# Attention decode with a gated feed-forward: V of a head in one transfer with 48 KB a partition, K in halves of the same rows

## The chip, the core and the metric

The kernel runs on one core of one Trainium2 chip. A core has a matrix engine (TensorE, PE in the profile), a vector engine (VectorE, DVE), a scalar engine (ScalarE, ACT), GpSimd (POOL) and a sync engine (SyncE, SP), which here only issues DMA transfers. Sixteen DMA engines carry data from the device memory into the on-chip memory of 128 partitions. The metric is the device time of one execution in microseconds.

## What is computed

One token of width 640 goes through a layer norm, multi-head attention over a cache, a residual, a second layer norm, a gated feed-forward layer and a second residual, all in float32:

```python
B, Sq, D = 1, 1, 640
H, Sk, Dh = 32, 8192, 192          # F = 1536
q = (layernorm(x) @ wq).reshape(B, Sq, H, Dh).transpose(0, 2, 1, 3)
scores = einsum("bhqd,bhkd->bhqk", q, k_cache) * Dh ** -0.5
o = einsum("bhqk,bhkd->bhqd", softmax(scores), v_cache)
h = x + o.transpose(0, 2, 1, 3).reshape(B, Sq, H * Dh) @ wo
n = layernorm(h)
gate = n @ W_gate
out = h + (gate * (gate > 0) * (n @ W_up)) @ W_down
```

K and V of one head are 8192 x 192 numbers each, 6.3 MB. The whole input is 446 MB, nearly all of it K and V, and each byte of them is used once.

## The kernel before

**Layout.** A head's 8192 cache positions are cut into two chunks of 4096 (`NCH = 2`). In a chunk each of the 128 partitions holds 32 positions that follow each other (`R = 32`), so a chunk is one tile of 128 rows of 24 KB, and each row is one contiguous piece of memory. `load_kv` (L77 to L83) loads such a chunk of K or V with one transfer of 3072 KB; the very last chunk of V comes in four quarters. All these tiles, the five slices of the query weights at the start and the feed-forward weights at the end share the pool `kv` with six buffers. The output weights have their own pool `wts` with two buffers.

**Start.** SP asks for the five slices of the query weights (L74). ACT asks for x twice: once with five numbers in each partition (`xT`), once as one row (`xrow`). After the layer norm, PE computes all 32 queries (L159), and ACT copies them out (`q4`). Four matmuls with a row of ones (L149) put x into the accumulator `acc`, as the residual.

**One head.** `query(h)` spreads the query of a head over all partitions in PSUM (L168). `scores_of` (L171) multiplies each half of a K chunk with it on DVE, in place (L178), and sums over the 192 columns: ten positions of each sixteen on DVE (L179), six on ACT (L181). `softmax_of` (L185) finds the maximum over all partitions with a transposition (L189) and a broadcast (L193) on PE, takes the exponential on ACT (L198) and sums with a matmul (L200). `values_of` (L212) multiplies with V: 32 matmul pairs of 384 columns, which the trace shows as 64 matmul records (L217); the first half of them reads V's chunk 0, the second chunk 1. ACT scales the result (L220). `to_columns` (L223) turns it so that it can be multiplied with the output weights, with matmuls (L232) and a transposition on DVE (L235). Heads go in groups: seven groups of four (0 to 27), then 28 and 29, then 30 and 31. When a group is complete, `output_of` (L237) multiplies with the output weights of the group and adds into `acc` (L241); the last two heads do so one by one.

**The loop** (L246 to L266) is software-pipelined by one head. In its pass h stand, in this order: at the first head of a group, the load of the group's output weights (`load_wo`, L90); the loads of K(h+1) chunk 0, V(h) chunk 0, K(h+1) chunk 1, V(h) chunk 1; the query of head h+1; the values of head h; scores and softmax of head h+1; `to_columns` of head h; and at the end of a group `output_of`.

**What sets the order.** All large loads are issued by SP on one queue. Each waits on SP until its buffer is free: for a K buffer, until DVE and ACT have summed the chunk that was in it; for a V buffer, until PE has multiplied it; for the output weights, until the last matmul of `output_of` that read the buffer. A load that waits keeps those behind it waiting. The transfers that are issued run on the 16 DMA engines, each engine taking 8 of the 128 rows of every transfer. The framework that builds the kernel places the instructions on each engine's queue and puts in the waits; for a pool with n buffers, the (n+1)th tile waits for the first to be released.

**End.** After the last head come the feed-forward weights (L275 to L290): up in two transfers, gate in three, down in four, in the same six buffers. Meanwhile PE, ACT and DVE finish `acc`, take the second layer norm (L293 to L313), compute up and gate (`project`, L315), combine and turn them (L329, L331) and compute the down projection in twelve slices as they land (L337). Two queues store the result (L343).

Of the kernel before, what the change touches and what calls it, by code (L numbers as in the profile page):

```python
# [7 lines left out]
F32 = mybir.dt.float32  # L8
# [6 lines left out]
def kernel(  # L15
# [23 lines left out]
    TW = R * DH  # L39
# [3 lines left out]
    DG = D // NQ  # L43
# [21 lines left out]
    xrow = const.tile([1, D], F32, name="xrow")  # L65
    nc.scalar.dma_start(xT, x[0, 0].rearrange("(p j) -> p j", p=P))
    nc.scalar.dma_start(xrow, x[0])


    wq_v = wq.rearrange("(p j) n -> p j n", p=P)  # L70
    wq_ts = []
    for j in range(DJ):
        t = kv.tile([P, TW], F32, name="kv_t")
        nc.sync.dma_start(t, wq_v[:, j, :])  # L74
        wq_ts.append(t)

    def load_kv(src, h, c, parts=1):  # L77
        t = kv.tile([P, TW], F32, name="kv_t")
        v = src[h, c * P * R:(c + 1) * P * R, :].rearrange("(p r) d -> p (r d)", p=P)
        n = TW // parts  # L80
        for i in range(parts):
            nc.sync.dma_start(t[:, i * n:(i + 1) * n], v[:, i * n:(i + 1) * n])
        return t  # L83

    def load_wo(gi):
        hs = GROUPS[gi]
        j = len(hs) * DH // P
        t = wts.tile([P, j, D], F32, tag="wo_t", name="wo_t")
        r0 = hs[0] * DH
        nc.sync.dma_start(t, wo[r0:r0 + len(hs) * DH, :].rearrange("(p j) n -> p j n", p=P))  # L90
        return t

    ones = const.tile([P, P], F32, name="ones")
# [3 lines left out]
    ident = const.tile([P, P], F32, name="ident")  # L97
# [73 lines left out]
    def scores_of(q, kts):  # L171
        sc = small.tile([P, NS], F32, name="sc")
        for c, kt in enumerate(kts):
            k3 = kt.rearrange("p (r d) -> p r d", d=DH)
            for r0 in range(0, R, SUB):
                ks = k3[:, r0:r0 + SUB, :]
                i0 = c * R + r0
                nc.vector.tensor_mul(ks, ks, q[:, None, :].to_broadcast([P, SUB, DH]))  # L178
                nc.vector.reduce_sum(sc[:, i0:i0 + SUB - NA], ks[:, :SUB - NA, :], axis=AX.X)  # L179
# [29 lines left out]
        nc.vector.memset(po, 0.0)  # L209
    NP = NS // 2  # L210

    def values_of(h, p, rl, vts):  # L212
        po = pos[h % 2]
        for i in range(NP):
            c, r = divmod(2 * i, R)
            g = i % NQ
            nc.tensor.matmul(po[g * Q:g * Q + 2, :], p[:, 2 * i:2 * i + 2],  # L217
                             vts[c][:, r * DH:(r + 2) * DH], start=(i < NQ), stop=(i >= NP - NQ))
        ob = small.tile([P, 2 * DH], F32, name="ob")
        nc.scalar.activation(ob, po, AF.Copy, scale=rl)  # L220
        return ob
# [19 lines left out]
                nc.tensor.matmul(acc[g * Q:(g + 1) * Q, :], oT[s, j, :], wo_t[s, j, g * DG:(g + 1) * DG],  # L241
                                 start=False, stop=(last and j == J - 1))

    kts = [load_kv(kf, 0, c) for c in range(NCH)]
    sm = softmax_of(scores_of(query(0), kts))
    for h in range(H):  # L246
        gi, i = group_of[h]
        hs = GROUPS[gi]
        if i == 0:
            wo_t = load_wo(gi)  # L250
            oT = small.tile([P, len(hs) * DH // P, Q], F32, tag="oT", name="oT")
        vts, kts = [], []
        for c in range(NCH):
            if h + 1 < H:
                kts.append(load_kv(kf, h + 1, c))
            vts.append(load_kv(vf, h, c, 4 if h == H - 1 and c == NCH - 1 else 1))
        if h + 1 < H:
            q = query(h + 1)
        ob = values_of(h, *sm, vts)
# [20 lines left out]
    up_b, gt_b = rest[:, 0:F], rest[:, F:2 * F]  # L280
    dn_b = rest[:, 2 * F:2 * F + 3 * D].rearrange("p (j n) -> p j n", n=D)
    dn_c = dn_a[:, 0:9 * D].rearrange("p (j n) -> p j n", n=D)
    nc.sync.dma_start(up_a, rows_of(w_up)[:, 0:JA, :])
    nc.sync.dma_start(up_b, rows_of(w_up)[:, JA, :])
    nc.sync.dma_start(gt_a[:, 0:2, :], rows_of(w_gate)[:, 0:2, :])
    nc.sync.dma_start(gt_a[:, 2:4, :], rows_of(w_gate)[:, 2:4, :])
    nc.sync.dma_start(gt_b, rows_of(w_gate)[:, JA, :])
# [24 lines left out]
    hr = row.tile([P, 1], F32, name="hr")  # L312
    rstd_of(hr, hvar, "h")  # L313

    def project(ps, wa, wb):  # L315
        for j in range(DJ):
            w = wa[:, j, :] if j < JA else wb
# [5 lines left out]
    project(pu, up_a, up_b)  # L323
# [3 lines left out]
    project(pg, gt_a, gt_b)  # L327
# [6 lines left out]
    for j in range(FJ):  # L334
        w = dn_b[:, j, :] if j < 3 else dn_c[:, j - 3, :]
        for g in range(NQ):
            nc.tensor.matmul(pd[g * Q:(g + 1) * Q, 0:DG], guT[:, j, :], w[:, g * DG:(g + 1) * DG],  # L337
                             start=(j == 0), stop=(j == FJ - 1))
# [32 lines left out]
```

## Time and profile before

| | |
|---|---|
| median of 3 runs | 1055.49 us (1055.3 to 1055.65) |
| the profiled execution | 1055.67 us, of which 1053.9 us is the span from the first to the last instruction |
| instructions | 8860 |
| granted TensorE clock, mean | 0.669 |
| data packets and bytes | 22374 packets, 446.48 MB, 424 GB/s over the span |

The page of the profile gives the busy time of each engine, then the span in 40 slices of 26.3 us with the busy share of the DMA engines and the GB/s that they moved, then the DMA queues, then the chain of work that ended last. Two more views are used. The DMA view can be cut to a stretch of time and then gives the packets, bytes and mean rate in it ("under 512 B" counts the short packets that report a transfer's completion, one for each of the 16 engines that took part). The timeline gives, for each instruction or run of equal ones, start, duration, engine, line, operation, tiles and shape, "x" and the count, and in brackets how long the engine had been idle before and what ended that. "SPq" marks SP's issue of a transfer. In the table of windows the last two numbers of a line are the DMA engines' busy share and the GB/s.

### The profile page before, as it was taken

To read this page: it belongs to the slowest core of one execution; us is meant where nothing else is said; L and a number is where in the kernel's file an instruction comes from. 1 tells how busy PE (TensorE), PEld (TensorE's weight loads), DVE (VectorE), ACT (ScalarE), POOL (GpSimd) and SP (SyncE) were. 2 spreads that over 40 slices of the span, in tenths; PEclk is the share of its full clock that TensorE was granted. 3 is DMA by queue.
4 is the path that set the end of the run, shared out by engine and by line. 5 is a ranking of instruction groups with operands and counts; after the bars stand their busy time and mean duration, and the time that the engine had idled before them with its cause. 6 is when DMAs were issued, how large, how long until landed. Compare 5 with 4: busy or idle time off the path is not lost.

```text
span 1053.9 us, 8860 instructions
## 1 busy us (share of the span) xinstructions
PE 439.4 (42%) x3136; PEld 135.6 (13%) x3136; DVE 727.0 (69%) x418; ACT 325.1 (31%) x1676; POOL 1.9 (0%) x11
## 2 busy tenths in 40 slices
PE   3523444344434333433442444344325433532466
PEld 1101111111111010111110111111101101100122
DVE  1188877677867777687776777677875877687641
ACT  0043333223323332232232333233332333333230
POOL 0000000000000000000000000000000000000000
PEclk9656666666676666766666665766667666666666
DMA  9999999999999999999999999999999999999995
GB/s 391 431 428 432 433 430 430 427 431 428 430 431 430 430 430 428 431 429 431 429 430 430 432 431 429 428 428 430 431 429 433 430 428 427 435 428 429 431 418 231
DMA packets 22374, 446.48 MB, mean 424 GB/s; under 512 B 2613, under 2 KB 2617, under 8 KB 4154
## 3 DMA queue, kind: packets, MB, share of 16 engines
q1 hardware_dynamic: 22180, 445.92, 99.0%
q8 instruction: 24, 0.39, 0.2%
q14 instruction: 20, 0.16, 0.0%
q10 hardware_dynamic: 150, 0.01, 0.0%
HBM read 445.91 MB, written 0.00 MB: 423 GB/s over the span
## 4 chain that ended last, share of the span: by engine, by line
DMA 62%; DVE 28%; PE 8%; issue 1%; ACT 1%; SPq 0%; DVEq 0%
DMA kv_t<-in_A_k_cache_dram 57%; DVE kv_t L178 19%; DVE sc L179 7%; PE po L217 5%; DMA up_a<-in_B_W_up_dram 3%; DMA dn_a<-in_B_W_down_dram 2%; PE q L168 1%; PE ps_small L232 1%; ACT p L198 0%; PE ps_small L193 0%; PE ps_small L200 0%; DVE oT L235 0%; DVE m L191 0%; SPq L74 0%; PE ps_small L189 0%
## 5 line engine op out<-in xcount | busy, mean ns | idle before, releaser
L178 DVE TENSOR_TENSOR kv_t<-kv_t,q 128x3072 f32<-128x3072 f32 x128 | 423.3, 3347 | 165.7 <-DMA kv_t<-in_A_k_cache_dram 165.1
L181 ACT ACTIVATE kv_t<-kv_t 128x192 f32<-128x192 f32 x768 | 267.7, 349 | 528.8 <-DVE kv_t L178 528.8
L217 PE MATMUL po<-kv_t,p 128*2 128x384 f32 x2048 | 296.7, 749 | 249.1 <-DMA kv_t<-in_A_v_cache_dram 249.1
L179 DVE TENSOR_REDUCE sc<-kv_t 128x10 f32<-128x1920 f32 x128 | 269.0, 2142 | 0.0
L168 PE MATMUL q<-q,sel 128*128 128x192 f32 x64 | 31.0, 589 | 285.6 <-DVE kv_t L178 285.6
L181 ACT ACTIVATION_READ_ACCUMULATOR kv_t<-kv_t 128x1 f32 x768 | 143.3, 187 | 0.0
L217 PEld LDWEIGHTS po<-kv_t,p 128*2 128x2 f32 x2048 | 60.5, 111 | 453.0 <-DMA kv_t<-in_A_v_cache_dram 274.6
L168 PEld LDWEIGHTS q<-q,sel 128*128 128x128 f32 x64 | 15.6, 303 | 316.5 <-DVE kv_t L178 242.2
L220 ACT ACTIVATE ob<-po,rl 128x384 f32<-128x384 f32 x32 | 18.6, 580 | 111.8 <-PE po L217 111.8
L202 DVE RECIPROCAL rl<-ps_small 128x1 f32<-128x1 f32 x32 | 5.4, 168 | 52.6 <-PE ps_small L200 52.6
L191 DVE TENSOR_REDUCE m<-ps_small 1x1 f32<-1x128 f32 x32 | 8.9, 279 | 40.5 <-PE ps_small L189 40.5
L235 DVE STREAM_TRANSPOSE oT<-ps_small 32x192 f32<-32x192 f32 (+1 forms) x32 | 11.7, 367 | 27.0 <-PE ps_small L232 27.0
L232 PE MATMUL ps_small<-ob,par 128*32 128x192 f32 (+1 forms) x144 | 25.6, 314 | 0.7 <-ACT ob L220 0.7
L159 PE MATMUL qp<-kv_t,xn 128*32 128x512 f32 x120 | 21.0, 862 | 11.1 <-DMA kv_t<-in_A_wq_dram 10.1
L200 PE MATMUL ps_small<-rs,ones 128*128 128x1 f32 x64 | 12.4, 264 | 24.9 <-ACT p L198 24.9
L241 PE MATMUL acc<-wo_t,oT 128*32 128x160 f32 (+1 forms) x408 | 18.2, 330 | 4.6 <-DVE oT L235 4.6
L193 PE MATMUL ps_small<-m,ones 1*128 1x1 f32 x64 | 12.3, 259 | 11.9 <-DVE m L191 11.9
L241 PEld LDWEIGHTS acc<-wo_t,oT 128*32 128x32 f32 (+1 forms) x408 | 13.2, 119 | 9.3 <-DVE oT L235 7.8
L200 PEld LDWEIGHTS ps_small<-rs,ones 128*128 128x128 f32 x64 | 9.7, 191 | 27.6 <-ACT p L198 27.6
L193 PEld LDWEIGHTS ps_small<-m,ones 1*128 1x128 f32 x64 | 9.6, 186 | 18.2 <-DVE m L191 18.2
L232 PEld LDWEIGHTS ps_small<-ob,par 128*32 128x32 f32 x144 | 11.3, 109 | 4.8 <-ACT ob L220 1.4
L198 ACT ACTIVATE p<-sc,nb 128x64 f32<-128x64 f32 x32 | 11.1, 348 | 1.2 <-ACT nb L195 0.2
(77 smaller groups left out, 80.3 us busy)
## 6 DMA issues: line engine op xcount, KB each, us to landing
kv_t<-in_A_k_cache_dram SPq DMA_DIRECT2D x64, 3072.0 KB, 33.7
kv_t<-in_A_v_cache_dram SPq DMA_DIRECT2D x63, 3072.0 KB, 39.8
kv_t<-in_A_wq_dram SPq DMA_DIRECT2D x5, 3072.0 KB, 13.9
wo_t<-in_A_wo_dram SPq DMA_DIRECT2D x7, 1920.0 KB, 41.5
kv_t<-in_A_v_cache_dram SPq DMA_DIRECT2D x4, 768.0 KB, 38.8
up_a<-in_B_W_up_dram SPq DMA_DIRECT2D x1, 3072.0 KB, 33.9
gt_a<-in_B_W_gate_dram SPq DMA_DIRECT2D x2, 1536.0 KB
dn_a<-in_B_W_down_dram SPq DMA_DIRECT2D x3, 960.0 KB, 22.7
```

The lines of the kernel that those rows point to most:

```text
L159: nc.tensor.matmul(qps[b][g * Q:(g + 1) * Q, :], xn[:, j:j + 1].to_broadcast([P, Q]), wq_ts[j][:, c0:c0 + QB], start=(j == 0), stop=(j == ...
L168: nc.tensor.matmul(q[:, 0:DH], sel[:, g, :], q4[:, i * DH:(i + 1) * DH], start=True, stop=True)
L178: nc.vector.tensor_mul(ks, ks, q[:, None, :].to_broadcast([P, SUB, DH]))
L179: nc.vector.reduce_sum(sc[:, i0:i0 + SUB - NA], ks[:, :SUB - NA, :], axis=AX.X)
L181: nc.scalar.activation(ks[:, r, :], ks[:, r, :], AF.Copy, accum_out=sc[:, i0 + r:i0 + r + 1])
L193: nc.tensor.matmul(pb[:, 0:1], ones[0:1, :], m1, start=True, stop=True)
L200: nc.tensor.matmul(pl[:, 0:1], ones, rs, start=True, stop=True)
L217: nc.tensor.matmul(po[g * Q:g * Q + 2, :], p[:, 2 * i:2 * i + 2], vts[c][:, r * DH:(r + 2) * DH], start=(i < NQ), stop=(i >= NP - NQ))
L220: nc.scalar.activation(ob, po, AF.Copy, scale=rl)
L232: nc.tensor.matmul(pt[q0:q0 + Q, 0:W], par[:, k, :], ob[:, k * DH + u * W:k * DH + (u + 1) * W], start=(k == 0), stop=(k == 1))
L235: nc.vector.transpose(oT[s], pt[s, 0:W].rearrange("p (c j) -> p j c", c=Q))
L241: nc.tensor.matmul(acc[g * Q:(g + 1) * Q, :], oT[s, j, :], wo_t[s, j, g * DG:(g + 1) * DG], start=False, stop=(last and j == J - 1))
```

## The change

V gets the layout of a whole head: each partition holds 64 positions that follow each other, 48 KB in one row, and one transfer of 6144 KB fetches them. The value matmuls read the same position pairs out of one tile. K must match the positions of V, so a K tile is now the first or the second half (24 KB) of the same 48 KB row. The pool `kv` of six 24 KB buffers becomes `kp` with three 24 KB buffers and `vp` with two 48 KB buffers; V's last head comes as one half and four quarters. The loads stand in the order K(h+1) half 0, K(h+1) half 1, V(h).

The query weights come as two transfers of two slices (48 KB a partition) in the `vp` buffers and one single slice in a `kp` buffer. The up weights come as one transfer of 30 KB a partition, the gate weights as 18 KB and 12 KB.

The pool of the output weights has one buffer in place of two. The load of a group moves from the group's first head to its third (`i == 2`); for the group of heads 28 and 29 it stands at the top of head 28, for the last group behind the load of V(30).

The residual x is loaded as four rows of 160 numbers and enters `acc` through four matmuls that select a row with a column of the identity, in place of a row of ones.

```diff
-    kv = ctx.enter_context(tc.tile_pool(name="kv", bufs=6))
-    wts = ctx.enter_context(tc.tile_pool(name="wts", bufs=2))
+    kp = ctx.enter_context(tc.tile_pool(name="kp", bufs=3))
+    vp = ctx.enter_context(tc.tile_pool(name="vp", bufs=2))
+    wts = ctx.enter_context(tc.tile_pool(name="wts", bufs=1))
...
-    nc.scalar.dma_start(xrow, x[0])
+    nc.scalar.dma_start(xq[0:NQ, :], x[0].rearrange("o (g n) -> (o g) n", g=NQ))
...
-    for j in range(DJ):
-        t = kv.tile([P, TW], F32, name="kv_t")
-        nc.sync.dma_start(t, wq_v[:, j, :])
-        wq_ts.append(t)
-
-    def load_kv(src, h, c, parts=1):
-        t = kv.tile([P, TW], F32, name="kv_t")
-        v = src[h, c * P * R:(c + 1) * P * R, :].rearrange("(p r) d -> p (r d)", p=P)
-        n = TW // parts
-        for i in range(parts):
-            nc.sync.dma_start(t[:, i * n:(i + 1) * n], v[:, i * n:(i + 1) * n])
+    for j in range(0, DJ, 2):
+        n = min(2, DJ - j)
+        t = vp.tile([P, 2 * TW], F32, name="v_t") if n == 2 else kp.tile([P, TW], F32, name="k_t")
+        t3 = t.rearrange("p (j n) -> p j n", n=TW)
+        nc.sync.dma_start(t3, wq_v[:, j:j + n, :])
+        wq_ts += [t3[:, i, :] for i in range(n)]
+
+    def load_k(h, c):
+        t = kp.tile([P, TW], F32, name="k_t")
+        nc.sync.dma_start(t, kf[h].rearrange("(p r) d -> p (r d)", p=P)[:, c * TW:(c + 1) * TW])
+        return t
+
+    def load_v(h, parts=1):
+        t = vp.tile([P, 2 * TW], F32, name="v_t")
+        v = vf[h].rearrange("(p r) d -> p (r d)", p=P)
+        b = 0
+        for n in parts:
+            nc.sync.dma_start(t[:, b:b + n], v[:, b:b + n])
+            b += n
         return t
...
-        nc.tensor.matmul(acc[g * Q:(g + 1) * Q, :], ones[0:1, 0:Q], xrow[:, g * DG:(g + 1) * DG],
+        nc.tensor.matmul(acc[g * Q:(g + 1) * Q, :], ident[0:NQ, g:g + 1].to_broadcast([NQ, Q]), xq[0:NQ, :],
                          start=True, stop=False)
...
             nc.tensor.matmul(po[g * Q:g * Q + 2, :], p[:, 2 * i:2 * i + 2],
-                             vts[c][:, r * DH:(r + 2) * DH], start=(i < NQ), stop=(i >= NP - NQ))
+                             vt[:, 2 * i * DH:(2 * i + 2) * DH], start=(i < NQ), stop=(i >= NP - NQ))
...
         if i == 0:
+            oT = small.tile([P, len(hs) * DH // P, Q], F32, tag="oT", name="oT")
+        if i == 2 or h == 28:
             wo_t = load_wo(gi)
-            oT = small.tile([P, len(hs) * DH // P, Q], F32, tag="oT", name="oT")
-        vts, kts = [], []
-        for c in range(NCH):
-            if h + 1 < H:
-                kts.append(load_kv(kf, h + 1, c))
-            vts.append(load_kv(vf, h, c, 4 if h == H - 1 and c == NCH - 1 else 1))
+        kts = [load_k(h + 1, c) for c in range(NCH)] if h + 1 < H else []
+        vt = load_v(h, [2 * TW] if h + 1 < H else [TW] + [TW // 4] * 4)
+        if h == 30:
+            wo_t = load_wo(gi)
         if h + 1 < H:
             q = query(h + 1)
...
-    JA = 4
-    up_a = kv.tile([P, TW], F32, tag="kv_t", name="up_a").rearrange("p (j n) -> p j n", n=F)
-    gt_a = kv.tile([P, TW], F32, tag="kv_t", name="gt_a").rearrange("p (j n) -> p j n", n=F)
-    dn_a = kv.tile([P, TW], F32, tag="kv_t", name="dn_a")
-    rest = kv.tile([P, TW], F32, tag="kv_t", name="rest")
...
-    nc.sync.dma_start(up_a, rows_of(w_up)[:, 0:JA, :])
-    nc.sync.dma_start(up_b, rows_of(w_up)[:, JA, :])
-    nc.sync.dma_start(gt_a[:, 0:2, :], rows_of(w_gate)[:, 0:2, :])
-    nc.sync.dma_start(gt_a[:, 2:4, :], rows_of(w_gate)[:, 2:4, :])
-    nc.sync.dma_start(gt_b, rows_of(w_gate)[:, JA, :])
+    JA = DJ - 3
+    big = vp.tile([P, 2 * TW], F32, tag="v_t", name="ffn_a")
+    gt_b = kp.tile([P, TW], F32, tag="k_t", name="gt_b")[:, 0:JA * F].rearrange("p (j n) -> p j n", n=F)
+    dn_c = kp.tile([P, TW], F32, tag="k_t", name="dn_c")[:, 0:9 * D].rearrange("p (j n) -> p j n", n=D)
+    up = big[:, 0:DJ * F].rearrange("p (j n) -> p j n", n=F)
+    gt_a = big[:, DJ * F:(DJ + 3) * F].rearrange("p (j n) -> p j n", n=F)
+    dn_b = kp.tile([P, TW], F32, tag="k_t", name="dn_b")[:, 0:3 * D].rearrange("p (j n) -> p j n", n=D)
+    nc.sync.dma_start(up, rows_of(w_up))
+    nc.sync.dma_start(gt_a, rows_of(w_gate)[:, 0:3, :])
+    nc.sync.dma_start(gt_b, rows_of(w_gate)[:, 3:DJ, :])
     nc.sync.dma_start(dn_b, rows_of(w_down)[:, 0:3, :])
```

More of the change, by code (lines that the diff above doesn't have):

```diff
@@ L64 @@
     xT = const.tile([P, DJ], F32, name="xT")
-    xrow = const.tile([1, D], F32, name="xrow")
+    xq = const.tile([Q, DG], F32, name="xq")
     nc.scalar.dma_start(xT, x[0, 0].rearrange("(p j) -> p j", p=P))
-    nc.scalar.dma_start(xrow, x[0])
+    nc.scalar.dma_start(xq[0:NQ, :], x[0].rearrange("o (g n) -> (o g) n", g=NQ))
     wq_v = wq.rearrange("(p j) n -> p j n", p=P)
     wq_ts = []
-    for j in range(DJ):
-        t = kv.tile([P, TW], F32, name="kv_t")
-        nc.sync.dma_start(t, wq_v[:, j, :])
-        wq_ts.append(t)
-    def load_kv(src, h, c, parts=1):
-        t = kv.tile([P, TW], F32, name="kv_t")
-        v = src[h, c * P * R:(c + 1) * P * R, :].rearrange("(p r) d -> p (r d)", p=P)
-        n = TW // parts
-        for i in range(parts):
-            nc.sync.dma_start(t[:, i * n:(i + 1) * n], v[:, i * n:(i + 1) * n])
+    for j in range(0, DJ, 2):
[15 more added lines that the diff above has]
+            b += n
         return t
@@ L242, in output_of @@
                                  start=False, stop=(last and j == J - 1))
-    kts = [load_kv(kf, 0, c) for c in range(NCH)]
+    kts = [load_k(0, c) for c in range(NCH)]
     sm = softmax_of(scores_of(query(0), kts))
@@ L273, in rows_of @@
         return w.rearrange("(p j) n -> p j n", p=P)
-    JA = 4
-    up_a = kv.tile([P, TW], F32, tag="kv_t", name="up_a").rearrange("p (j n) -> p j n", n=F)
-    gt_a = kv.tile([P, TW], F32, tag="kv_t", name="gt_a").rearrange("p (j n) -> p j n", n=F)
-    dn_a = kv.tile([P, TW], F32, tag="kv_t", name="dn_a")
-    rest = kv.tile([P, TW], F32, tag="kv_t", name="rest")
-    up_b, gt_b = rest[:, 0:F], rest[:, F:2 * F]
-    dn_b = rest[:, 2 * F:2 * F + 3 * D].rearrange("p (j n) -> p j n", n=D)
-    dn_c = dn_a[:, 0:9 * D].rearrange("p (j n) -> p j n", n=D)
-    nc.sync.dma_start(up_a, rows_of(w_up)[:, 0:JA, :])
-    nc.sync.dma_start(up_b, rows_of(w_up)[:, JA, :])
-    nc.sync.dma_start(gt_a[:, 0:2, :], rows_of(w_gate)[:, 0:2, :])
-    nc.sync.dma_start(gt_a[:, 2:4, :], rows_of(w_gate)[:, 2:4, :])
-    nc.sync.dma_start(gt_b, rows_of(w_gate)[:, JA, :])
+    JA = DJ - 3
[8 more added lines that the diff above has]
+    nc.sync.dma_start(gt_b, rows_of(w_gate)[:, 3:DJ, :])
     nc.sync.dma_start(dn_b, rows_of(w_down)[:, 0:3, :])
@@ L313, with project @@
     rstd_of(hr, hvar, "h")
-    def project(ps, wa, wb):
+    def project(ps, row_of):
         for j in range(DJ):
-            w = wa[:, j, :] if j < JA else wb
+            w = row_of(j)
             for g in range(NQ):
@@ L322 @@
     pu = ps_q.tile([P, QB], F32, tag="q", name="pu")
-    project(pu, up_a, up_b)
+    project(pu, lambda j: up[:, j, :])
     us = row.tile([P, FG], F32, name="us")
@@ L326 @@
     pg = ps_q.tile([P, QB], F32, tag="q", name="pg")
-    project(pg, gt_a, gt_b)
+    project(pg, lambda j: gt_a[:, j, :] if j < 3 else gt_b[:, j - 3, :])
     gu = row.tile([P, FG], F32, name="gu")
```

5 lines of the change are left out of this document (2 added, 3 removed).

## The prediction

> **What bounds the kernel now.** I read the page from the top, then the chain that ended last, then the DMA view cut to two windows.
>
> ```profile
> PE 439.4 (42%) x3136; PEld 135.6 (13%) x3136; DVE 727.0 (69%) x418; ACT 325.1 (31%) x1676; POOL 1.9 (0%) x11
> GB/s 391 431 428 432 433 430 430 427 431 428 430 431 430 430 430 428 431 429 431 429 430 430 432 431 429 428 428 430 431 429 433 430 428 427 435 428 429 431 418 231
> q1 hardware_dynamic: 22180, 445.92, 99.0%
> DMA 62%; DVE 28%; PE 8%; issue 1%; ACT 1%; SPq 0%; DVEq 0%
> ```
>
> The busiest compute engine, DVE, works 69% of the span. The DMA engines are busy 99.0% of it on the one queue that carries the data, and every slice but the first and the last two moves 427 to 435 GB/s. The chain's 28% on DVE only shows whose work freed a buffer for the next load: the loads stand in line behind others anyway. So the time is 445.92 MB at about 430 GB/s, and an edit counts in two ways only: it changes the time that the engines need for the bytes, or it makes the queue run dry.
>
> ```profile
> DMA packets 12060, 257.99 MB, mean 430 GB/s; under 512 B 1338, under 2 KB 1338, under 8 KB 1338
> q1 hardware_dynamic: 12036, 257.68, 100.3%
> DMA packets 536, 4.24 MB, mean 424 GB/s; under 512 B 56, under 2 KB 56, under 8 KB 378
> q1 hardware_dynamic: 536, 4.24, 101.5%
> ```
>
> These are the DMA view's packet lines for 300 to 900 us (almost all 24 KB rows) and for 1026 to 1036 us (feed-forward weights in 6 to 12 KB rows). **What a packet costs.** In the first there are 12036 - 1338 = 10698 data packets of 24.09 KB (thousand bytes) on average; at 430/16 = 26.9 GB/s an engine, 0.896 us each. In the second 480 packets of 8.83 KB at 26.5 GB/s, 0.333 us each. The straight line through both has 36.9 ns per KB and an intercept of 7 ns; with the busy shares (100.3% and 101.5%) in place of the rates it is 13 ns. I take 10 ns for each packet that goes away, and 7 and 13 as ends.
>
> **The change, part by part: fewer packets.**
>
> ```profile
> kv_t<-in_A_v_cache_dram SPq DMA_DIRECT2D x63, 3072.0 KB, 39.8
> kv_t<-in_A_v_cache_dram SPq DMA_DIRECT2D x4, 768.0 KB, 38.8
> kv_t<-in_A_wq_dram SPq DMA_DIRECT2D x5, 3072.0 KB, 13.9
> gt_a<-in_B_W_gate_dram SPq DMA_DIRECT2D x2, 1536.0 KB
> ```
>
> A transfer has 128 rows, 8 for each engine. V goes from 63 whole transfers and 4 quarters to 31 of double rows, one half and 4 quarters: (63 - 32) x 8 = 248 packets fewer per engine. The query weights go from 5 transfers to 3: 16 fewer. Up goes from 2 to 1, gate from 3 to 2: 8 fewer each. That is 280 x 10 ns = 2.8 us. The transfers themselves fall by 31 + 2 + 1 + 1 = 35, each with one small completion packet per engine; at between nothing and the same 10 ns this is 0 to 0.35 us, I take 0.2. **Sum: 3.0 us saved**, between 2.0 and 4.0 by the ends above. No run shows a 48 KB packet: if it is cut in two it saves nothing, so 0 is the lower end.
>
> Is there more to win from fewer transfers? The window of 300 to 900 us holds 1338/16 = 84 transfers and is 100.3% busy; half a per cent that the share hides would be 36 ns for each, 1.2 us for 35. The Trainium skill ("DMA: Bandwidth & Descriptors", section "Anatomy of one DMA") gives every DMA a fixed 2.0 us beside its bytes; an estimate by it for 35 fewer is 70 us saved where the rows give at most 1.2. This trace disagrees: 84 times 2.0 us would leave 168 of the 600 us idle, and none are.
>
> K in halves of one row reads 24 KB pieces out of 48 KB rows. The old gate transfers already read 12 KB out of 30 KB rows in the window at 424 GB/s, and the query weights 24 KB out of 120 KB rows in the first two slices, of which the second has 431: I take nothing.
>
> **Does the queue stay fed?**
>
> ```profile
> 876.24 6.62 DVE L178 TENSOR_TENSOR kv_t<-kv_t,q 128x3072 f32<-128x3072 f32 x2 [3.00 <-DMA kv_t<-in_A_k_cache_dram]
> 882.78 4.21 DVE L179 TENSOR_REDUCE sc<-kv_t 128x10 f32<-128x1920 f32 x2
> 890.92 6.62 DVE L178 TENSOR_TENSOR kv_t<-kv_t,q 128x3072 f32<-128x3072 f32 x2
> 898.18 5.15 PE L217 MATMUL po<-kv_t,p 128*2 128x384 f32 x32 [7.71 <-DMA kv_t<-in_A_v_cache_dram]
> 1015.73 6.98 PE L217 MATMUL po<-kv_t,p 128*2 128x384 f32 x64
> ```
>
> At 430 GB/s 3072 KB take 7.3 us, so a head takes 29.3: K, K, then V whole. Let K(h+1,0) land at 0; K(h+1,1) lands at 7.3, V(h) at 21.9. The 64 value matmuls of a head took 6.98 us where they ran in one piece (L217 x64), and stand in front of the softmax on PE's queue: they end at 29.4. DVE then needs the softmax (887.0 to 890.9, about 4 us) and 10.75 us per K half, so head h+1's first half is done near 14.5 and its second near 25.2. The third K buffer gives the first half's place to K(h+2,1), whose bytes are due at 29.3: 14 us in hand. K(h+3,0) has 25 us, V(h+1) 21 (issued right behind K(h+2,1)). The values now come later than before, and this margin hides it; without it, every microsecond would cost 32 times. Both margins I cost at nothing, this one and that of the first heads:
>
> ```profile
> 48.54 6.62 DVE L178 TENSOR_TENSOR kv_t<-kv_t,q 128x3072 f32<-128x3072 f32 x2 [32.84 <-DMA kv_t<-in_A_k_cache_dram]
> 55.08 4.21 DVE L179 TENSOR_REDUCE sc<-kv_t 128x10 f32<-128x1920 f32 x2
> ```
>
> K(0,0) is scored from 48.5 to 59.3, and K(1,1) needs its buffer. K(0,0) landed near 48, so K(0,1) and K(1,0) last until 48 + 2 x 7.3 = 62.6; with 1.0 us from issue to bytes (below) there are 2 us in hand.
>
> The output weights of heads 0 to 27 are asked for two heads (58 us) after their one buffer is free, those of heads 30 and 31 behind V(30), 29.3 us after V(29), and the buffer is free 13 us after V(29) (below). **Heads 28 and 29 are different.** Their load stands at the top of head 28, in front of K(29,0), and its one buffer is held until the last output matmul of head 27. That needs V(27), the last transfer in front of it in the same queue. So SP waits with nothing behind V(27) in flight: the DMA engines run dry.
>
> ```profile
> 873.31 0.33 SPq L82 DMA_DIRECT2D kv_t<-in_A_k_cache_dram  x1
> 873.73 0.38 SPq L82 DMA_DIRECT2D kv_t<-in_A_v_cache_dram  x1
> 874.16 0.42 SPq L90 DMA_DIRECT2D wo_t<-in_A_wo_dram  x1
> 999.17 0.33 SPq L284 DMA_DIRECT2D rest<-in_B_W_up_dram  x1
> 1009.94 0.33 SPq L285 DMA_DIRECT2D gt_a<-in_B_W_gate_dram  x1
> 1015.67 0.33 SPq L287 DMA_DIRECT2D rest<-in_B_W_gate_dram  x1
> SPq L285 <- DVE sc L179: 10.4, 1, 10.4
> ```
>
> The queue keeps the order of the program even where a later load could go: gt_a waited 10.4 us for its buffer (SP's own waits) while L287, into a tile that was already placed at 999.17, stayed behind it; and wo_t at 874.16, whose second buffer was free, stands behind the K and V of the head before, which had waited.
>
> ```profile
> 912.14 1.01 PE L168 MATMUL q<-q,sel 128*128 128x192 f32 x2 [8.82 <-DVE kv_t L178]
> 913.08 4.53 PE L217 MATMUL po<-kv_t,p 128*2 128x384 f32 x32
> 920.92 1.84 PE L241 MATMUL acc<-wo_t,oT 128*32 128x160 f32 x48 [0.48 <-DVE oT L235]
> 0.74 2.96 SPq L74 DMA_DIRECT2D kv_t<-in_A_wq_dram  x5
> 0.00:1.00 1.00, 0.00 (x0) 0.00 (x0) 0.16 (x2) 0.00 (x0) 0.47 (x6) 1.00 0.00 0
> 1.00:2.00 1.00, 0.00 (x0) 0.00 (x0) 0.77 (x4) 0.24 (x1) 0.92 (x4) 1.00 1.16 295
> 2.00:3.00 1.00, 0.00 (x0) 0.00 (x0) 0.00 (x0) 1.00 (x1) 0.51 (x3) 1.00 0.43 98
> 1047.00:1048.00 1.00, 1.00 (x20) 0.77 (x16) 0.00 (x0) 0.00 (x0) 0.00 (x0) 0.50 0.06 23
> 1048.00:1049.00 1.00, 0.58 (x12) 0.02 (x3) 0.00 (x0) 0.00 (x0) 0.00 (x0) 0.50 0.04 15
> 1049.08 1.83 PE L337 MATMUL pd<-dn_a,guT 128*32 128x160 f32 x24 [0.50 <-DMA dn_a<-in_B_W_down_dram]
> ```
>
> **The price of the dry stretch**, from V(27)'s last byte to the next byte: landing to first matmul 0.5 us (the last bytes flow before 1049, PE starts at 1049.08); the 64 value matmuls 7.0 (two pieces of 5.15 would be 10.3, the upper end; one piece at the rate of the second half of 4.53 + 4.53 gives 9); from their end to the end of the output matmuls 922.76 - 917.61 = 5.15 (the softmax of head 28, the copy of the values, the transposition); SP's issue to the first byte 1.0 (issue at 0.74, bytes in the window from 1 to 2); and a slow restart: the window from 2 to 3 us moved 98 GB/s, so 0 to 1.4 us, I take 0.5. **Sum: 14.2 us**, between 11 and 18. Nothing hides it: the stream is the bound, everything behind it moves by as much. What is late next is K(29,0), and DVE with it. At the end only one engine of 16 still moves bytes (share 0.06 at 1047), so one engine lags; V(27) too has landed only when this one is done, so its full wait counts.
>
> **Start and end.** The query weights' pairs end with the single fifth transfer, which still lands fifth, and K(0,0) lands when it did. The 4-row matmul for x stands beside the weights' transfer. At the end up, gate and down follow V(31) in the old order with the same bytes; two gate rows come last in place of one, 8 matmuls or about 0.7 us more, in front of the first down group:
>
> ```profile
> 1042.29 1.21 PE L337 MATMUL pd<-rest,guT 128*32 128x160 f32 x24 [1.64 <-DVE guT L331]
> 1044.41 1.83 PE L337 MATMUL pd<-dn_a,guT 128*32 128x160 f32 x24 [0.91 <-DMA dn_a<-in_B_W_down_dram]
> ```
>
> The second group waits 0.91 us for its bytes, which covers it. Nothing.
>
> **Sum.** The profiled execution took 1055.67 us for a span of 1053.9; the median of the runs, 1055.49, is 0.02% lower, so I add to the median: 1055.5 - 3.0 + 14.2 = **1066.7 us**.
>
> **The rivals.** (1) *Faster*: the wait at head 28 doesn't empty the queue, because the order of issue comes out otherwise (K(29) in front of the output weights) or the buffer is free in time. It decides from the point where 14.2 us of bytes, two K halves, stand in front of that load. Then 1055.5 - 3.0 = 1052.5 us. Against it are the rows of SP's order; for it, only that PE's order does differ from the program's (the query of L168 at 912.14 stands between the two halves of a head's values). 10%. (2) 48 KB rows win nothing, because they are cut or run at the old rate: 1055.5 + 14.2 = 1069.7. 15%. (3) A margin fails too, for instance K(1,1)'s 2 us or a per-head one: it would cost from some 3 us once, 1070, to 32 us at 1 us a head. 5%. (4) Each transfer has a fixed gap of its own, and dropping 35 saves it 35 times: by the 1.2 us above 1065.5, inside my range and counted with the forecast. By the Trainium skill's 2.0 us for each, an estimate, it would be about 1000 us; under 1%.
>
> **How the numbers follow.** Forecast 69%, rivals as above. The range takes the gap's ends: 1055.5 - 4.0 + 11 = 1062.5 and 1055.5 + 18 = 1073.5; rival (1) lies outside with 10%. A difference of 0.2%, about 2 us, is what a measurement of this kernel can tell from no change. Faster by more 10%, within 3% (the gap hidden and the rows worth nothing), slower 87%.
>
> **What would show it.** One wait of SP at the output weights' load, over 30 us long, released by PE's output matmul; one slice of the GB/s line between 900 and 930 us at about half; the other slices 431 to 432; about 17,300 packets in place of 22374; DVE waiting some 25 us for K once. No dip, or several, make the prediction wrong, and so does a data rate in the middle that is below 430.

## The result, and the profile after

| | before | changed |
|---|---|---|
| median | 1055.57 us (4 runs) | 1164.15 us (4 runs, 1162.47 to 1165.67) |
| ratio, 95% interval | | 1.103 [1.1016, 1.1044] |
| span of the profiled execution | 1053.9 us | 1162.5 us |

The change costs 108.6 us. The forecast was 11 us slower: the direction is right, the size ten times too small, and the time lies far outside the range.

First the page of the changed kernel, in the parts that were quoted of before: busy times, GB/s in 40 slices (now of 29 us), the data queue, and the shares of the chain that ended last.

```profile
PE 402.4 (35%) x3136; PEld 143.8 (12%) x3136; DVE 723.8 (62%) x418; ACT 325.0 (28%) x1676; POOL 1.9 (0%) x11
GB/s 403 421 422 431 440 430 404 364 412 360 383 405 358 415 381 350 356 432 416 379 357 353 410 375 419 366 366 411 369 355 368 419 416 368 273 252 434 431 337 323
DMA packets 17340, 446.48 MB, mean 384 GB/s; under 512 B 2056, under 2 KB 2064, under 8 KB 3344
q1 hardware_dynamic: 17140, 445.92, 90.9%
DVE 61%; PE 27%; DMA 6%; ACT 3%; issue 2%; SPq 0%; DVEq 0%
```

The packets went as forecast (17340; forecast about 17,300), and no engine has much more to do than before: DVE is busy for 723.8 us (727.0 before), ACT for 325.0 (325.1), PE's matmuls for 402.4 (439.4); only PE's weight loads take a little longer (143.8 against 135.6). But from the seventh slice to the 34th the stream runs at 350 to 432 GB/s: a loss in every head. The single dip that was forecast is there as well, in the slices of 273 and 252, but it is not where the time went (e8 below). DMA had 62% of the chain that ended last; now it has 6%, and DVE and PE have 88%. So the kernel is no longer bound by the bytes, nor by the work of one engine (DVE is busy 62%), but by a chain that runs back and forth between engines. Two rows of the groups show where DVE stands idle in it, and that PE never waits for V:

```profile
L225 PE MATMUL po<-v_t,p 128*2 128x384 f32 x2048 | 248.4, 655 | 0.0
L243 DVE STREAM_TRANSPOSE oT<-ps_small 32x192 f32<-32x192 f32 (+1 forms) x32 | 11.7, 367 | 290.4 <-PE ps_small L240 290.4
```

DVE waits 290.4 us, on average 9.1 us in each of the 32 heads, in front of one small transposition, that of `to_columns` (L243; L235 before). In the kernel before, that idle time was 27.0 us in all:

```profile
L235 DVE STREAM_TRANSPOSE oT<-ps_small 32x192 f32<-32x192 f32 (+1 forms) x32 | 11.7, 367 | 27.0 <-PE ps_small L232 27.0
```

The chain that ended last, over one head of the changed kernel (start, duration, what):

```profile
433.00 0.23 DVE mp L196
...
435.34 0.58 PE ps_small L209 x2
435.92 7.82 PE po L225 x64
443.77 0.59 ACT ob L228
...
444.40 0.85 PE ps_small L240 x4
445.28 0.38 DVE oT L243
445.69 6.62 DVE k_t L187 x2
452.31 4.12 DVE sc L188 x2
456.43 6.53 DVE k_t L187 x2
462.96 4.14 DVE sc L188 x2
467.18 0.23 DVE mp L196
```

This is one ring, and nothing in it runs beside anything else: softmax 2.9 us, the 64 value matmuls 7.8, scaling and turning 1.9, two K halves on DVE 21.5; from maximum (`mp`) to maximum 467.18 - 433.00 = 34.18 us. The bytes of a head need 29.3. Two placements close the ring. On PE the values of head h stand **behind** the softmax of head h+1 (L225 begins when L209 ends; the V that it reads was asked for at 388.56 us, and a load of V here lands 18.8 to 40.4 us after its issue). On DVE the transposition that needs these values stands **in front of** the first multiplication of the next K half, which needs nothing of it.

The size follows from the times of the maxima. The view of one line gives the count, the durations in ns, and the start of the first and of the last; first of the kernel before, then of the changed one:

```profile
L187 DVE TENSOR_REDUCE mp<-sc x32: 219/220/222, 70.0 to 1010.0; 128x1 f32<-128x64 f32 x32
```

```profile
L196 DVE TENSOR_REDUCE mp<-sc x32: 211/220/220, 73.1 to 1115.1; 128x1 f32<-128x64 f32 x32
```

31 steps take 940.0 us before (30.3 each) and 1042.0 changed (33.6 each): 102 of the 108.6 us. (In the changed kernel the first step takes 18.8 us, and the 30 behind it some 34.1 each.) The rest is 3.1 us in front of the first maximum and 3.5 behind the last (47.4 against 43.9 us to the end of the span).

The wait that was forecast at head 28 is there, at 24.9 us (forecast over 30). SP's own waits for the output weights (us in total, times, longest), and SP's timeline around it:

```profile
SPq L99 <- PE acc L249: 48.1, 2, 24.9
```

```profile
979.10 23.87 SPq L82 DMA_DIRECT2D k_t<-in_A_k_cache_dram  x2
1027.91 0.33 SPq L99 DMA_DIRECT2D wo_t<-in_A_wo_dram  x1
1028.28 0.43 SPq L90 DMA_DIRECT2D v_t<-in_A_v_cache_dram  x1
```

But the two halves of K(29) were issued in front of it. The framework had moved them ahead, so SP's order is not the program's.

### The profile page after: what moved, and what is told of

Its sections match the earlier page's. It is cut to its first block, busy times and chain, and to the rows that moved or that the text cites. A ratio compares the mean times of both kernels' runs of the same rounds, so it can differ in the third digit from the quotient of the medians.

```text
span 1162.5 us, 8804 instructions
## 1 busy us (share of the span) xinstructions
PE 402.4 (35%) x3136; PEld 143.8 (12%) x3136; DVE 723.8 (62%) x418; ACT 325.0 (28%) x1676; POOL 1.9 (0%) x11
## 2 busy tenths in 40 slices
DMA packets 17340, 446.48 MB, mean 384 GB/s; under 512 B 2056, under 2 KB 2064, under 8 KB 3344
## 4 chain that ended last, share of the span: by engine, by line
DVE 61%; PE 27%; DMA 6%; ACT 3%; issue 2%; SPq 0%; DVEq 0%
DVE k_t L187 36%; DVE sc L188 23%; PE po L225 21%; DMA k_t<-in_A_k_cache_dram 4%; DMA dn_c<-in_B_W_down_dram 2%; PE ps_small L240 2%; PE ps_small L202 2%; PE ps_small L209 2%; ACT ob L228 2%; ACT p L207 1%; PE ps_small L198 1%; DVE oT L243 1%; DVE m L200 1%; DVE mp L196 1%; ACT nb L204 0%
## 5 line engine op out<-in xcount | busy, mean ns | idle before, releaser
L187 DVE TENSOR_TENSOR k_t<-k_t,q 128x3072 f32<-128x3072 f32 x128 | 422.9, 3342 | 26.1 <-DMA k_t<-in_A_k_cache_dram 25.4
L190 ACT ACTIVATE k_t<-k_t 128x192 f32<-128x192 f32 x768 | 267.6, 349 | 385.9 <-DVE k_t L187 385.9
L188 DVE TENSOR_REDUCE sc<-k_t 128x10 f32<-128x1920 f32 x128 | 269.0, 2141 | 0.0
L225 PE MATMUL po<-v_t,p 128*2 128x384 f32 x2048 | 248.4, 655 | 0.0
L243 DVE STREAM_TRANSPOSE oT<-ps_small 32x192 f32<-32x192 f32 (+1 forms) x32 | 11.7, 367 | 290.4 <-PE ps_small L240 290.4
L190 ACT ACTIVATION_READ_ACCUMULATOR k_t<-k_t 128x1 f32 x768 | 143.4, 187 | 0.0
L225 PEld LDWEIGHTS po<-v_t,p 128*2 128x2 f32 x2048 | 58.0, 103 | 168.1 <-issue 167.6
L198 PE MATMUL ps_small<-ident,mp 128*1 128x128 f32 x32 | 11.9, 372 | 146.6 <-DVE mp L196 146.6
L209 PE MATMUL ps_small<-rs,ones 128*128 128x1 f32 x64 | 18.7, 362 | 24.9 <-ACT p L207 24.9
L202 PE MATMUL ps_small<-m,ones 1*128 1x1 f32 x64 | 18.6, 357 | 13.4 <-DVE m L200 13.4
L209 PEld LDWEIGHTS ps_small<-rs,ones 128*128 128x128 f32 x64 | 16.0, 310 | 27.6 <-ACT p L207 27.6
L202 PEld LDWEIGHTS ps_small<-m,ones 1*128 1x128 f32 x64 | 15.8, 305 | 22.8 <-DVE m L200 22.8
## 6 DMA issues: line engine op xcount, KB each, us to landing
v_t<-in_A_v_cache_dram SPq DMA_DIRECT2D x31, 6144.0 KB, 25.4
```

The source lines that it names most:

```text
L190: nc.scalar.activation(ks[:, r, :], ks[:, r, :], AF.Copy, accum_out=sc[:, i0 + r:i0 + r + 1])
L198: nc.tensor.transpose(pt[0:1, 0:P], mp, ident)
L202: nc.tensor.matmul(pb[:, 0:1], ones[0:1, :], m1, start=True, stop=True)
L209: nc.tensor.matmul(pl[:, 0:1], ones, rs, start=True, stop=True)
L243: nc.vector.transpose(oT[s], pt[s, 0:W].rearrange("p (c j) -> p j c", c=Q))
```

## The experiments

**Theory A**: the time goes into that ring, which exists because the values stand behind the softmax on PE and the transposition ahead of the next K half on DVE. **Rivals**: the large rows or the few buffers starve the stream by themselves; or the wait at head 28 costs the time.

| run | time, us | ratio to before, 95% interval |
|---|---|---|
| e1 values first | 1055.51 | 1.000 [0.9991, 1.0009] |
| e2 transposition late | 1057.91 | 1.0021 [1.0012, 1.0031] |
| e3 kernel before, values last | 1134.01 | 1.0743 [1.0729, 1.0758] |
| e4 V in two transfers | 1055.66 | 1.0002 [0.9993, 1.0011] |
| e5 values first, output weights late | 1053.43 | 0.998 [0.9971, 0.9989] |
| e6 as e5, V in two transfers | 1055.82 | 1.0004 [0.9996, 1.0013] |
| e7 values first, output weights in front | 1069.95 | 1.0136 [1.0121, 1.0152] |
| e8 changed kernel, output weights late | 1163.63 | 1.1028 [1.1013, 1.1043] |
| e9 V between the K halves | 1056.92 | 1.0012 [1.0003, 1.0021] |
| e10 as e9, output weights late | 1052.72 | 0.9974 [0.9964, 0.9984] |

### e1 and e2: the ring cut at either end

The edit of e1 touches nothing but PE's order: the softmax of head h+1 may only be placed behind the last value matmul of head h.

```diff
...
-        ob = values_of(h, *sm, vt)
+        ob, mm = values_of(h, *sm, vt)
         if h + 1 < H:
-            sm = softmax_of(scores_of(q, kts))
+            sc = scores_of(q, kts)
+            with tc.issue_after(mm.ins if hasattr(mm, "ins") else mm):
+                sm = softmax_of(sc)
```

Here `mm` is the last value matmul.

> The changed kernel with one thing altered: on PE's queue the value matmuls of head h stand in front of the softmax of head h+1 again. Buffers, transfers and rows stay. Theory A (the loss is a chain through the order on PE and DVE: softmax, values, transposition, next K): DVE needs 21.3 + about 4 us a head, the chain falls below the 29.3 us that a head's bytes take, the stream is the bound again: 1052 to 1056 us. Theory B (three K buffers and two V buffers are too few for the queue): still 1150 us or more. Theory C (48 KB rows, or K as halves of such rows, move slower): still 1150 us or more, with the DMA engines busy throughout.

e2 leaves PE's order as it is in the changed kernel, and puts the transposition of head h on DVE behind the last multiplication of head h+2, where the changed kernel has it in front of the first one.

```diff
...
-            sm = softmax_of(scores_of(q, kts))
+            sc = scores_of(q, kts)
+            if 0 < h < H - 2:
+                tc.add_manual_dep(last_ot[0].ins, last_mul[0].ins.name, mybir.DependencyInfo(
+                    mybir.DependencyClass.NoSync, mybir.DependencyReason.DATA), reason="order")
+            sm = softmax_of(sc)
```

> The changed kernel with the other link of the chain cut: PE keeps the values behind the softmax, but on DVE the transposition of head h's output stands behind the last multiplication of the next head in line and no longer in front of its first. Theory A: DVE doesn't wait for the values any more, a head costs DVE about 26 us, so the stream is the bound: 1052 to 1060 us. Theory A' (what hurts is the late values alone, through V's buffers): 1110 us or more. Theories B and C: 1150 us or more.

e1 took 1055.51 us, e2 1057.91: either cut alone takes nearly the whole loss back. Of e1 first, then of e2, the GB/s line and DVE's group (L245 in e2 is the same transposition):

```profile
GB/s 391 429 430 439 423 421 433 432 429 437 441 421 439 419 431 429 437 429 430 433 428 430 432 432 436 429 428 425 433 432 431 432 438 429 395 374 432 434 424 307
L243 DVE STREAM_TRANSPOSE oT<-ps_small 32x192 f32<-32x192 f32 (+1 forms) x32 | 11.7, 365 | 22.8 <-PE ps_small L240 22.8
```

```profile
GB/s 395 426 429 438 429 424 431 430 429 445 425 436 425 426 431 431 430 435 432 434 423 430 431 433 434 431 437 423 427 431 431 430 443 423 438 290 431 426 415 303
L245 DVE STREAM_TRANSPOSE oT<-ps_small 32x192 f32<-32x192 f32 (+1 forms) x32 | 11.7, 365 | 25.4 <-PE ps_small L242 24.7
```

The idle time of 290.4 us falls to 22.8 and 25.4, and the stream is back at some 430 GB/s with the same rows, buffers and packets. What is left is one dip near the end, at the output weights. PE's timeline of e1 shows the values ahead of the softmax:

```profile
451.45 7.86 PE L225 MATMUL po<-v_t,p 128*2 128x384 f32 x64 [0.45 <-DMA v_t<-in_A_v_cache_dram]
459.24 0.27 PE L198 MATMUL ps_small<-ident,mp 128*1 128x128 f32 x1
```

They take as long as in the changed kernel (7.86 against 7.82 us), so it is their place that counts, and not a slower PE. On DVE the framework placed one multiplication of the next K half ahead of the transposition in seven of e1's heads; in all others DVE's order is that of the changed kernel, so there the order on PE alone opens the ring.

### e3: the ring put into the kernel before

The kernel before, with its 24 KB rows and six buffers, with the values of head h placed behind the softmax of head h+1.

```diff
...
-        ob = values_of(h, *sm, vts)
+        prev = sm
         if h + 1 < H:
             sm = softmax_of(scores_of(q, kts))
+        with tc.issue_after(last_pl[0].ins):   # the last matmul of softmax_of
+            ob = values_of(h, *prev, vts)
...
```

> The kernel before with its 24 KB rows, six buffers and order of loads, but with the values of a head behind the softmax of the next on PE's queue. Theory A: the same chain arises without any change of rows, 34 us a head: 1150 to 1180 us. Theories B and C: rows and buffers are those of before, so about 1056 us.

1134.01 us, ratio 1.0743 [1.0729, 1.0758]: 78 us from the order alone, with nothing else of the change, but below the 1150 to 1180 expected. Its GB/s line and the transposition:

```profile
GB/s 398 426 433 430 429 430 430 430 423 409 374 410 371 409 400 386 411 361 407 365 433 382 390 405 374 414 367 414 396 387 409 357 419 359 419 375 384 422 288 238
L237 DVE STREAM_TRANSPOSE oT<-ps_small 32x192 f32<-32x192 f32 (+1 forms) x32 | 11.7, 367 | 261.9 <-PE ps_small L234 261.9
```

Why it is less shows on DVE's timeline. In eight of the 31 steps from maximum to maximum the framework placed the first multiplication of the next K half (L178) in front of the transposition, so that part of it runs beside the values:

```profile
498.35 3.35 DVE L178 TENSOR_TENSOR kv_t<-kv_t,q 128x3072 f32<-128x3072 f32 x1
507.52 0.37 DVE L237 STREAM_TRANSPOSE oT<-ps_small 32x192 f32<-32x192 f32 x1 [5.82 <-PE ps_small L234]
```

Such a step takes 30.4 to 30.8 us; all others but the first (25.8) take some 34.1, as in the changed kernel. Eight times 3.3 us is 26 us. The mechanism holds; the size was put too high because it took the full ring for every head. The loss also begins some three slices later than in the changed kernel; that the six common buffers gave the stream a longer lead is an argument, no run shows it.

### e4: V in two transfers

```diff
-        vt = load_v(h, [2 * TW] if h + 1 < H else [TW] + [TW // 4] * 4)
+        vt = load_v(h, [TW] * 2 if h + 1 < H else [TW] + [TW // 4] * 4)
```

> The changed kernel with V in two transfers, each half of the 48 KB rows (24 KB), everything else the same; the order that is planned for PE then has the first half of the values in front of the softmax and the second behind it. Theory A: the chain loses the 3.5 to 4.5 us of one half, 34.2 down to about 30 us a head: 1052 to 1070 us. Theory B: the same buffers, so 1150 us or more. Theory C with K's halves as the cause: 1150 us or more; with V's 48 KB rows as the cause: about 1056 us.

1055.66 us. Now the framework places half of a head's values in front of the softmax and half behind it (timeline of PE):

```profile
449.00 3.74 PE L225 MATMUL po<-v_t,p 128*2 128x384 f32 x32
452.67 0.27 PE L198 MATMUL ps_small<-ident,mp 128*1 128x128 f32 x1
...
454.74 2.76 PE L225 MATMUL po<-v_t,p 128*2 128x384 f32 x32
```

Only the second half, 2.8 us, stays in the ring. Two transpositions that follow each other, on DVE's timeline:

```profile
430.32 0.39 DVE L243 STREAM_TRANSPOSE oT<-ps_small 32x192 f32<-32x192 f32 x1 [4.06 <-PE ps_small L240]
...
459.08 0.37 DVE L243 STREAM_TRANSPOSE oT<-ps_small 32x192 f32<-32x192 f32 x1 [4.06 <-PE ps_small L240]
```

The ring now takes 28.8 us, which is less than the 29.3 of the bytes, so the stream is the bound again, by half a microsecond a head.

### e8, e7 and e5: the output weights of heads 28 and 29

e8 is the changed kernel with the load of these weights behind V(28).

```diff
-        if i == 2 or h == 28:
+        if i == 2:
...
-        if h == 30:
+        if h in (28, 30):
```

> The changed kernel with only the output weights of heads 28 and 29 moved behind the load of V(28); PE's order stays that of the changed kernel. Theory A (the chain on DVE and PE sets the time, the queue has slack): SP's wait of 24.9 us costs nothing there, so 1161 to 1166 us. Rival (that wait is part of the loss): 1140 to 1150 us.

1163.63 us, 0.5 less than the changed kernel: the only term that the forecast added costs nothing there, since the stream has slack in every head. In the changed kernel the maxima around the wait are at 979.1, 1013.3 and 1047.5 us, 34.2 apart like the others. e7 builds the kernel that the prediction had in mind: values first as in e1, and K(29) and V(28) held behind the output weights on SP.

```diff
...
+        if h == 28:
+            with tc.issue_after(last_wo[0].ins):
+                kts = [load_k(h + 1, c) for c in range(NCH)]
+                vt = load_v(h, [2 * TW])
...
```

Here `last_wo[0]` is the load of the output weights.

> The kernel that the prediction had in mind: values first on PE, and on SP's queue the output weights of heads 28 and 29 in front of K(29) and V(28), so that nothing is behind V(27). Theory (the prediction's dry stretch of 14.2 us, fully on the path): 1064 to 1068 us. Rival (most of it is hidden, since the engines that run ahead only lose their lead): 1056 to 1060 us.

e5 is e1 with e8's edit: values first and no dry stretch.

> Values first on PE (as in the run with values first) and the output weights of heads 28 and 29 asked for behind V(28), where their buffer has long been free. The wait at head 28 left the DMA engines idle for about 4.9 us on average in that run (910 to 930 us). Theory A (the wider rows save 2.7 us of DMA work, and the wait gave it back): 1051.5 to 1053.5 us, faster than before by 0.2 to 0.4%. Rival (the saved work is lost elsewhere): about 1055.5.

e7 took 1069.95 us, 2 more than the 1064 to 1068 expected of it, and e5 1053.43: the dry stretch alone is 16.5 us (forecast 14.2, between 11 and 18). It lies where it was forecast. Of e7, windows of 5 us (the last two numbers: DMA share, GB/s), then PE's timeline, then SP's:

```profile
910.00:915.00 5.00, 3.98 (x26) 0.88 (x29) 3.82 (x3) 1.70 (x10) 0.00 (x0) 0.50 0.00 2
915.00:920.00 5.00, 4.63 (x47) 1.20 (x39) 0.28 (x1) 0.58 (x1) 0.00 (x0) 0.86 0.02 3
920.00:925.00 5.00, 3.79 (x56) 2.79 (x56) 0.56 (x2) 0.61 (x3) 0.00 (x0) 0.82 0.00 0
```

```profile
911.56 7.71 PE L227 MATMUL po<-v_t,p 128*2 128x384 f32 x64 [1.02 <-DMA v_t<-in_A_v_cache_dram]
922.58 2.88 PE L251 MATMUL acc<-wo_t,oT 128*32 128x160 f32 x48 [0.48 <-DVE oT L245]
```

```profile
925.50 0.33 SPq L101 DMA_DIRECT2D wo_t<-in_A_wo_dram  x1
```

V(27) lands near 911.5; values 7.7 us (forecast 7.0); from their end to the end of the output matmuls 925.46 - 919.27 = 6.2 (forecast 5.15, the matmuls took 2.9 and not 1.84). In e1, where the two halves of K(29) stand in front of this load, the same wait costs 2.1 us (e1 less e5).

### e6: the rows of V

e5 with V in two transfers, the edit of e4.

> The same as the version with values first and late output weights, but V in two transfers of 24 KB a partition. Prices V's 48 KB rows alone: 248 packets and 31 transfers more for each engine. By the durations in the traces (two packets of 914 ns against one of 1818, and 9 ns for each completion) 2.5 to 2.8 us more than with 48 KB rows: 1054 to 1056 us. Rival (rows are worth nothing): the same time as with 48 KB rows.

1055.82 us, 2.4 more than e5 (2.5 to 2.8 expected). 31 transfers and 248 packets an engine fewer are worth 2.4 us; if all of it is put to the packets, 9.6 ns each (forecast 10).

### e9 and e10: V between the K halves

Why did the framework place the values last? e9 leaves V whole and changes only the order of the loads.

```diff
-        kts = [load_k(h + 1, c) for c in range(NCH)] if h + 1 < H else []
+        kts = [load_k(h + 1, 0)] if h + 1 < H else []
         vt = load_v(h, [2 * TW] if h + 1 < H else [TW] + [TW // 4] * 4)
+        if h + 1 < H:
+            kts.append(load_k(h + 1, 1))
```

> The changed kernel with the loads of a head in the order K half 0, V, K half 1; V stays one transfer of 48 KB rows. On PE's queue the framework then puts the 64 value matmuls of a head in front of the query and the softmax of the next one, with nothing said by hand, and on SP the output weights of heads 28 and 29 stand behind K half 0 of head 29 and V of head 28. Theory A (the time went into a chain through PE and DVE, which exists only where the values stand behind the softmax; its cause is V's place at the end of a head's loads, not its row length): no chain, 1052 to 1056, about 1053.5 as the kernel with values first and the output weights late, mp to mp 29.3 us. Rival B (48 KB rows, or two V buffers and three K buffers, are too few to keep the stream fed): 1100 or more, SP waiting for V's buffer in every head. A third way: V now wants its buffer 7.3 us earlier against the release of V two heads before; if that is too early it shows as SP's wait at V's load with the DMA share below 99%.

1056.92 us: no ring, with nothing said of PE's order by hand (at 903.46 us the 64 values of a head begin, at 924.93 the next softmax), but 0.9 us above the expected range. The slice of 270 GB/s in its GB/s line, SP's waits at the output weights, and SP's timeline show why:

```profile
GB/s 399 426 431 431 437 429 432 424 427 434 433 437 427 428 433 426 430 432 433 437 427 433 423 432 432 432 434 434 429 428 431 424 433 432 435 270 432 432 424 317
```

```profile
SPq L99 <- PE acc L249: 73.9, 8, 41.2
```

```profile
934.46 0.33 SPq L99 DMA_DIRECT2D wo_t<-in_A_wo_dram  x1
```

The output matmuls of head 27 here stand behind the softmax of head 28, so the weights' load waited until 934.46, longer than the loads in front of it lasted. e10 asks for the weights one load later, behind the second half of K(29).

> The kernel of e9 (loads of a head in the order K half 0, V, K half 1) with the output weights of heads 28 and 29 asked for one load later, behind K half 1 of head 29. In e9 they waited until 934.46 us for the output matmuls of head 27, which stand behind the softmax of head 28 on PE, and the engines had run dry by then: mean share 0.25 in 925 to 930 and 0.02 in 930 to 935, 9.8 us of lost share in 920 to 940 in all. Theory A, as mended by e9 (only that wait sets e9 apart from the kernel with values first and the output weights late, and it costs what the last of the 16 engines loses, 3.4 us): the slice of 270 GB/s goes and the time is 1053 to 1054. Rival (the order K, V, K costs something in every head, for instance at V's buffers): 1056 to 1057 as e9, without the dip. A third way: K half 1 of head 29 has to wait for its buffer longer than the output weights did, and the dip stays: 1056 or more.

Its GB/s line:

```profile
GB/s 395 426 432 433 442 422 440 418 428 433 437 431 440 420 427 430 431 432 437 429 434 427 426 433 432 434 436 426 431 429 428 429 437 433 428 398 423 417 428 282
```

1052.72 us, ratio 0.9974 [0.9964, 0.9984]; the slice of 270 is at 398. The time is 0.3 us below the 1053 to 1054 expected and near that of rival (1), 1052.5. It is the fastest kernel of this study, 0.3% below the kernel before; e5 is 0.2% below it. The order K, V, K itself costs nothing.

## Why the prediction was wrong

**The step that failed** is in "Does the queue stay fed?": the 64 value matmuls "stand in front of the softmax on PE's queue: they end at 29.4". In the changed kernel they stand behind it. From this sentence came the 14 us in hand for K and the term of nothing for every head. The margin itself was real: e1, with the assumed order, runs at some 430 GB/s in every head but the one with the dip. It was a margin of buffers, though, and what failed is an order. The row of before that the step leaned on showed half of a head's values ahead of the next query and half between query and softmax; how they would be placed when V's shape and place change was not in the trace, and the step took it as known. It should have had a price as a rival: 7 us of values, 4 of softmax and 21.5 of K on DVE were all in the rows used, and put end to end they make 32.5 us against 29.3, even without scaling and turning.

**"The queue keeps the order of the program"** failed too: K(29) was issued ahead of the output weights. That was rival (1), given 10%. In the changed kernel it decided nothing (e8), while in e1 it is why the wait costs 2.1 and not 16.5 us.

**The dry stretch** was right as a mechanism (e7: 16.5 us) and wrong as a forecast of this kernel, in which it costs nothing (e8). Its lower end of 11 us does not come out of the terms listed, whose ends add up to 13.65 and 18.35. With both assumed orders in force the kernel takes 1069.95 us, 3.3 from the forecast of 1066.7 and inside its range.

**The packets** were right: 3.0 us forecast, 2.0 (e5) and 2.9 (e10) measured against the runs of before. Rival (2), 48 KB rows that win nothing, falls with e6. So does rival (4) with its 2.0 us for each transfer. The Trainium skill ("DMA: Bandwidth & Descriptors", section "Anatomy of one DMA") states a fixed 2.0 us beside the bytes for a DMA that GpSimd issues, and puts most of it down to the wait for completion; here SP issues the loads, so the prediction applied it more widely than that section does. Paid by each of e6's 31 more transfers it would be an estimate of 62 us; the measured 2.4 us show that this full queue does not pay it each time.

**Rival (3)**, "a margin fails too", at 5%, named the form that came true, a price in every head; its upper end was 32 us at 1 us a head. The price was 3.3 us a head (33.6 less 30.3), over three times that. One of the signs that the prediction named against itself, "a data rate in the middle that is below 430", is what the page of the changed kernel shows.

**What stays open** is by what rule the framework orders the values. e4 and e9 show that it follows the loads: with the first half of V alone the first half of the values comes first, and with V ahead of the second K half all of them do. Whether it goes by a reckoned landing time or by the order of the loads as such was not tried.

## What to carry to other kernels

When an edit changes the shape or place of a load, read the new order of the compute engines before trusting any margin taken from the old trace: list, for each engine that takes its work in order, what stands behind what. Then add up the ring that these orders can close (here 7.8 + 1.9 + 21.5 + 2.9 us) and compare it with the time of the bytes. Here the longer ring was paid in every round, though no compute engine was busy for more than 62% of the span, and cutting it at either one of two places was enough.

## What the runs showed of the hardware

**A small transfer beside large rows.** x (20 bytes a partition, on ACT's queue) lands later in the changed kernel. The DMA issues of before in the first 12 us, and of the changed kernel in the first 20 us (the last number is us from issue to landing):

```profile
xT<-in_A_x_dram ACTq DMA_DIRECT2D x1, 2.5 KB, 10.7
```

```profile
xT<-in_A_x_dram ACTq DMA_DIRECT2D x1, 2.5 KB, 18.1
```

That is 7.4 us more for the same 8 rows an engine. At 26.9 GB/s an engine a 24 KB row takes 0.91 us and a 48 KB row 1.83, and 8 x 0.91 = 7.3: each small packet seems to wait for one large one of the other queue. The Trainium skill ("DMA: Bandwidth & Descriptors", section "Queues, rings and completion order") says that an engine takes turns between its queues packet by packet; these two times agree. No run varied it by itself. It cost nothing, since the first K half was scored from 48.54 us before and from 48.55 in the changed kernel.

**These dry stretches cost less than their lost share.** Windows of 5 us (the last two numbers: DMA share, GB/s), of e9 and then of e10:

```profile
920.00:925.00 5.00, 0.07 (x1) 0.07 (x1) 5.00 (x4) 0.17 (x1) 0.00 (x0) 0.50 0.82 354
925.00:930.00 5.00, 2.39 (x9) 1.53 (x9) 5.00 (x3) 2.62 (x15) 0.00 (x0) 0.50 0.25 108
930.00:935.00 5.00, 4.52 (x58) 2.62 (x60) 3.00 (x4) 2.18 (x12) 0.00 (x0) 0.51 0.02 10
```

```profile
920.00:925.00 5.00, 0.13 (x1) 0.08 (x1) 5.00 (x4) 0.23 (x1) 0.00 (x0) 0.50 0.92 398
925.00:930.00 5.00, 2.40 (x9) 1.53 (x8) 5.00 (x3) 2.56 (x15) 0.00 (x0) 0.50 0.96 413
930.00:935.00 5.00, 4.52 (x70) 2.52 (x72) 2.94 (x4) 2.18 (x12) 0.00 (x0) 0.70 0.67 258
```

e9 loses 9.6 us of mean share in these 15 us, e10 2.3, and the times differ by 4.2 us, not 7.3. From 900 to 930 us e7 loses 22.0 us and e5 none, and the times differ by 16.5. In e7 the 16 engines do not run out together: their mean share is 0.68 from 900 to 905 us and 0.14 from 905 to 910, and some bytes still move from 910 to 911. That only what the last one loses counts is an inference, and no run shows it alone.
